# Re-ordering the hand-written start of a fused linear-attention and MLP kernel: unit order, fences, a split weight conversion and load order

## The chip, the cores and the metric

The kernel runs on one core of one Trainium2 chip. The metric is device time in microseconds (us); before the change the median of nine runs is 604.74 us (603.56 to 607.88). Engines are named as in the profile: PE is the matrix engine, PEld its weight loads, DVE the vector engine, ACT the scalar engine, POOL GpSimd, SP the engine that here only issues DMAs.

## What is computed

Two blocks one after the other, in float32:

```python
# r, k, v, w: (4, 8, 768, 48); u: (8, 48); state: (B, H, 48, 48), zero at first
for t in range(S):
    cur = einsum('bhd,bhe->bhde', u[None] * k[:, :, t], v[:, :, t])
    y[:, :, t] = einsum('bhd,bhde->bhe', r[:, :, t], state + cur)
    state = w[:, :, t][:, :, :, None] * state + einsum('bhd,bhe->bhde', k[:, :, t], v[:, :, t])
x = y.transpose(0, 2, 1, 3).reshape(3072, 384)
h = x @ w_in                                  # (3072, 2048)
out = (0.5 * h * (1 + erf(h / sqrt(2)))) @ w_out   # (3072, 384)
```

The two weight matrices arrive as 64-bit floats. The kernel converts them itself to 32-bit floats while it runs.

## The kernel before

**Tiles.** The 3072 tokens are eight tiles of 384, numbered x = 0 to 7. For each tile `attention(x, unit)` makes the tile's 384 x 384 input of the MLP, transposed (`xT`), and `mlp(x)` makes the tile's output. Tile 0 is cut into two units, each with half of the heads, so that work can start when half of its data is in; unit 0 is called U0 here and unit 1 U1. Every later tile is one unit. While the MLP of tile x - 1 runs on PE, the attention of tile x is woven into it.

**How the order is made.** Nothing is scheduled by a tool: the order of the Python calls is the order of the instructions on every engine. `attention` and `mlp` are generators. Each `next` on an attention emits one slot: slot 0 products with u (ACT, L367) and products of the decays (DVE, L377), slots 1 and 2 the level h = 1, slots 3 to 7 the levels h = 2, 4, 8, 16, 32, slot 8 the transposes of k (PE L572, copied by ACT L574), slot 9 the products k v (PE L598), then the part of y inside a chunk (PE L639), the chain of states (DVE L618 and L613), and the part of y from the states (PE L677). A level is a block of products `d` on PE (L408), a product on DVE that changes r and k in place (L443), and a masked copy of `d` into `a_sb` (DVE L453; for h = 16 and 32 ACT L450). A level's `d` needs the r and k that the level before it left. Between L639 and L677 stand the fences (L649 and L651): tiny DVE copies of the last columns of y, which make what follows wait for the first set of y products.

The units of tile 0 take turns: slots 0 to 2 for U0 and then U1, and then one slot for each in turn. From slot 8 on U1 goes first (`units.reverse()`). After slot 8 come one whole conversion, and then nine hand-ordered steps, (0, 0, 1, 0, 0, 1, 1, 0, 1), where 0 stands for U1 and 1 for U0. `keep_warm(n)` puts n bfloat16 matmuls of zeros on PE (L196), whose results nobody uses.

**End of tile 0.** U1's y goes to `xT` in two ways: one pair of heads is copied to `ysb` by ACT (L703) and spread by six small DMAs (L707, three on ACT's queue and three on SP's), the other by two DVE copies (L700). U0's y is copied by ACT and DVE (L684). When all of these are in, the first matmul of `mlp(0)` (L874, `h_ps`) can start.

**Weights.** Each matrix is cut into eight pieces of 768 values per partition: pieces 0 to 7 are of `w_in`, pieces 8 to 15 of `w_out` (called o0 to o7 here). A piece is loaded raw (five buffers), `prepare` makes its two halfway forms f and e on ACT (L297, L298; two buffers each), and `finish` makes the 32-bit weights with four DVE instructions (L309, L311, L312, L316). `conversion` does one piece: it prepares the piece after it, finishes its own, and issues the load of a further one. Two matmul steps of `mlp(0)` use one piece: steps 0 to 15 are the sixteen blocks of h (L874), two to a piece, and steps 16 to 31 the sixteen blocks of the output product of two row groups (L1011), block f of it at step 16 + f, with piece o0 for f = 0 and 1 and so on to o7 for f = 14 and 15.

**mlp(0) with attention(1).** For tile 1 three hand-written lists set the order by step: conversions after steps 0, 2, 4, 6, 8, 10, 12, 14, 15, 17, 18, 20, 22, 24; attention slots after steps 1, 3, 5, 7, 9, 11, 13 (levels), 15 (transposes), 18 (k v), 20 (the chain, twenty L613), 26 (L639 and fences), 32 (L677). In one step the conversion is emitted ahead of the slot. Two conversions stand ahead of step 0, so piece o5 (blocks f = 10 and 11) is converted after step 20, ahead of the chain that is emitted at the same step.

**Loads at the start.** SP issues tile 0's data first. `shares` then hands out loads slot by slot, each held back by a one-column DVE memset of its target (L130, L174): weight piece 0 in three parts, tile 1's r, k and w in eight shares (`load_second`), tile 1's v, then pieces 1 and 2 in three parts each. Piece 3 is loaded by the first conversion and piece 4 by the second.

The tile-1 step lists in the code:

```python
place = [1, 3, 5, 7, 9, 11, 13, 15, 18, 20, 26, 32] if x == 1 else [1, 6, 8, 13, 15, 16, 18, 18, 20, 21]
...
if x == 1 and step in (0, 2, 4, 6, 8, 10, 12, 14, 15, 17, 18, 20, 22, 24):
    convert()
```

Of the kernel before, what the change touches and what calls it, by code (L numbers as in the profile page):

```python
# [36 lines left out]
HALFWAY = 2  # L37


def as_float(bits):  # L40
    return struct.unpack("<f", struct.pack("<I", bits))[0]
# [3 lines left out]
def kernel(  # L45
# [25 lines left out]
    nc = tc.nc  # L71
# [25 lines left out]
    def units_of(x):  # L97
        return NPART if x == 0 else 1
# [22 lines left out]
    def load_v(x, dma):  # L121
        loaded[x][1] = io.tile([128, v.shape[2]], F32, name="v_in")
        dma.dma_start(out=loaded[x][1], in_=v[x])

    def load_second(dma):

        loaded[1] = [None, None]
        for i in range(SHARES):
            s = slice(i * 3 * ALL // SHARES, (i + 1) * 3 * ALL // SHARES)
            nc.vector.memset(bufs[1][:, s.start:s.start + 1], 0.0)  # L130
            dma.dma_start(out=bufs[1][:, s], in_=rkw[1, :, s])
            yield
        load_v(1, dma)
        yield

    def load(x, dma):

        if x >= NX:
            return
        loaded[x] = [None, None]  # L140
        for i in range(3):
            if i == 1:
                load_v(x, dma)
                yield
            t = bufs[x % 2 if i == 0 else 1]
            for j in range(3):
                a = i * ALL + j * ALL // 3
                dma.dma_start(out=t[:, a:a + ALL // 3], in_=rkw[x, :, a:a + ALL // 3])
                yield
# [12 lines left out]
    def weight_in(gate=False):  # L162

        if len(raws) < len(pieces):
            dst, src = pieces[len(raws)]
            raws.append(cv.tile([128, PIECE], I64, name="raw", bufs=AHEAD) if wide else None)
            if wide:
                dst = raws[-1].rearrange("p (a c) -> p a c", a=dst.shape[1])
            if not gate:
                nc.sync.dma_start(out=dst, in_=src)  # L170
                return
            for i in range(dst.shape[1]):
                if wide:
                    nc.vector.memset(dst[:, i].bitcast(U32)[:, 0:1], 0)  # L174
                nc.sync.dma_start(out=dst[:, i], in_=src[:, i])
                yield
# [13 lines left out]
    def keep_warm(n, elsewhere=False):  # L190
        if elsewhere:
            t = pd.tile([128, 2, BANK], F32, name="warm", tag="d")[:, 0]
        else:
            t = ps.tile([128, BANK], F32, name="warm", tag="mm", bufs=2)
        for _ in range(n):
            nc.tensor.matmul(t, lhsT=zeros[:, 0:128], rhs=zeros, start=True, stop=True)  # L196
# [72 lines left out]

    halfway, converted = [], [0]  # L270

    def conversion():

        i = converted[0]
        if i >= len(pieces):
            return
        converted[0] += 1

        prepare(i + HALFWAY)
        if wide:  # L280
            yield from finish(pieces[i][0], raws[i], *halfway[i])
        for _ in weight_in():
            pass

    def convert():
        for _ in conversion():
            pass

    def prepare(upto):
        if not wide:  # L290
            return
        for i in range(len(halfway), min(upto, len(raws))):
            words = raws[i].bitcast(U32).rearrange("p (a b) -> p a b", b=2)
            lo, hi = words[:, :, 0], words[:, :, 1]
            f = cv.tile([128, PIECE], U32, name="f")
            e = cv.tile([128, PIECE], U32, name="e")
            nc.scalar.activation(out=f.bitcast(F32), in_=hi.bitcast(F32), func=AF.Abs)  # L297
            nc.scalar.activation(out=e.bitcast(F32), in_=lo, func=AF.Identity, scale=2.0 ** -51, bias=two)  # L298
            halfway.append((f, e))

    def finish(dst, raw, f, e):

        hi = raw.bitcast(U32).rearrange("p (a b) -> p a b", b=2)[:, :, 1]

        nc.vector.tensor_scalar(out=f.bitcast(F32), in0=f.bitcast(F32), scalar1=as_float(0x38000000),  # L309
                                scalar2=as_float(0x47EFFFFF), op0=ALU.max, op1=ALU.min)  # L310
        nc.vector.tensor_scalar(out=f, in0=f, scalar1=3, scalar2=None, op0=ALU.logical_shift_left)  # L311
        nc.vector.scalar_tensor_tensor(out=e, in0=hi, scalar=0x80000000, in1=e,  # L312
                                       op0=ALU.bitwise_and, op1=ALU.bitwise_or)
        yield
        f, e = (z.rearrange("p (a c) -> p a c", a=dst.shape[1]) for z in (f, e))
        nc.vector.tensor_tensor(out=dst.bitcast(U32), in0=f, in1=e, op=ALU.add)  # L316
# [3 lines left out]
    def attention(x, unit):  # L320
# [288 lines left out]
        def chain_states():  # L609
            for c in range(NC - 1 + int(first)):  # L610
                if c or not first:
                    for q in range(qs):
                        nc.vector.scalar_tensor_tensor(out=stq[:, q, c], in0=stq[:, q, c - 1] if c else b4[:, q, NC - 1],  # L613
                                                       scalar=totq[:, q, c:c + 1], in1=kvs[q // Q][:, q % Q, c // 2, c % 2],
                                                       op0=ALU.mult, op1=ALU.add)
                else:
                    for b in range(np_):
                        nc.vector.tensor_copy(out=stq[:, b * Q:(b + 1) * Q, c], in_=kvs[b][:, :, 0, 0])  # L618
# [24 lines left out]
        def fences():  # L643

            for y, y_ps in ys:
                fence = wk.tile([128, 2], F32, name="fence")
                if split:
                    for c in range(2):
                        nc.vector.tensor_copy(out=fence[:, c:c + 1], in_=y[c][:, NI * C - 1:NI * C])  # L649
                else:  # L650
                    nc.vector.tensor_copy(out=fence, in_=y_ps[:, :, NI * C - 1])  # L651

        if x == 0:

            inside()
            yield
            chain_states()
            yield
            fences()
        else:  # L660
            chain_states()
            yield
            inside()
            fences()
            yield
# [44 lines left out]
    N_SLOTS = len(LEVELS) + 7  # L710
# [310 lines left out]


    units = [attention(0, unit) for unit in range(units_of(0))]
    second = load_second(nc.sync)
    shares = chain(weight_in(gate=True), second, weight_in(gate=True), weight_in(gate=True))
    for unit in units:
        for _ in range(3):
            next(unit)
# [3 lines left out]
    for slot in range(3, N_SLOTS - 4):  # L1032
        for _ in range(2):
            next(shares, None)
        if slot == N_SLOTS - 7:
            prepare(1)
        if slot == N_SLOTS - 5:

            units.reverse()
        for unit in units:  # L1040
            next(unit)
            keep_warm(2)
    for _ in shares:
        pass
    convert()

    for unit in (0, 0, 1, 0, 0, 1, 1, 0, 1):
        next(units[unit])
    keep_warm(6, True)
    convert()  # L1050
# [5 lines left out]
    for x in range(1, NX):  # L1056

        place = [1, 3, 5, 7, 9, 11, 13, 15, 18, 20, 26, 32] if x == 1 else [1, 6, 8, 13, 15, 16, 18, 18, 20, 21]
        place_next = [38, 47] if x == 1 else [21, 24] if x % 2 == 0 else [25, 27]
        loads = load(x + 1, nc.scalar if x > 1 else nc.sync)  # L1060

        times = range(20, 30) if x == 1 else (2, 3, 4, 5, 16, 17, 18, 19, 20, 21)
        following = attention(x + 1, 0) if x + 1 < NX else iter(())
        more = iter(())
        for step, _ in enumerate(mlp(x - 1)):
            if x == 1 and step == 2 * NF - 2:

                make_quarter_masks()
                more = w_sums()
            next(more, None)  # L1070
            if x == 1 and step in (0, 2, 4, 6, 8, 10, 12, 14, 15, 17, 18, 20, 22, 24):
                convert()
            if step in times:
                next(loads, None)
            while place and place[0] <= step:
                place.pop(0)
                next(slots, None)
            while place_next and place_next[0] <= step:
                place_next.pop(0)
                next(following, None)  # L1080
            if x == NX - 1:

                if step == 18:
                    more_h = h_sums()
                for _ in range({18: 1, 22: 2, 25: 1}.get(step, 0)):
                    next(more_h)
        for _ in slots:
            pass
        slots = following
# [62 lines left out]
```

## Time and profile before

| what | value |
|---|---|
| median of nine runs | 604.74 us |
| time of the profiled execution | 605.13 us |
| its span, first to last instruction | 603.3 us |
| PE busy | 587.2 us (97%) |
| DVE busy | 468.4 us (78%) |
| ACT busy | 178.9 us (30%) |
| granted PE clock | 1.000 |
| 31.6 to 45.5 us: PE, DVE, ACT busy | 9.37, 9.73, 5.14 of 13.90 us |
| 45.5 to 91.4 us: PE, DVE, ACT busy | 44.62, 45.02, 28.06 of 45.90 us |
| 91.4 to 115.6 us: PE, DVE, ACT busy | 24.20, 23.60, 10.47 of 24.20 us |
| 115.6 to 603.0 us: PE, DVE, ACT busy | 484.35, 363.12, 125.34 of 487.40 us |

All times of events count from the first instruction of the profiled execution. The first stretch is the end of tile 0's attention. The second holds the h matmuls of tile 0 with the levels of tile 1, the third the output matmuls of tile 0's first two row groups. The last stretch is all the rest. In the profile's own time lines a row has start, duration, engine, line, operation and tiles, a count, and in brackets the idle time of the engine before it with what ended that time.

### The profile page before, as it was taken

Reading aid. Unit: us, or ns where it says so; the run is one execution under the profiler, and the core shown is the slowest. Engines: PE = TensorE matmul, PEld = TensorE weight load, DVE = VectorE, ACT = ScalarE, POOL = GpSimd, SP = SyncE. Lnnn points to the kernel's source line nnn. Section 1 sums busy time; section 2 is a strip of 40 time slices with the busy share of each in tenths; the row PEclk is TensorE's granted clock in tenths of the full one; section 3 lists DMA queues with packets and bytes.
Section 4 is the critical chain, followed back from the end, with each engine's and each line's share of the span. In section 5 each row is a group of like instructions: output and inputs, shape, how many; then the busy total and the mean of one; then the engine's idle time right before and its main releaser. Section 6 shows DMA issues by size and latency. Waiting matters only on the chain.

```text
span 603.3 us, 16117 instructions
## 1 busy us (share of the span) xinstructions
PE 587.2 (97%) x6993; PEld 455.5 (76%) x7008; DVE 468.4 (78%) x896; ACT 178.9 (30%) x414; POOL 8.4 (1%) x24
## 2 busy tenths in 40 slices
PE   8769999999999999999999999999999999999997
PEld 4556666656699568986699568995789668999977
DVE  8969999998875978588884988679786888665701
ACT  2336477023222322203322232113222133024400
POOL 3100000000000000000000000000000000000000
PEclk9999999999999999999999999999999999999999
DMA  5767348002052304203052303313042002010000
GB/s 198 233 200 251 108 157 304 33 28 84 8 109 75 92 2 110 73 21 93 1 112 73 98 1 75 93 36 92 3 107 67 17 1 40 14 39 8 1 14 26
DMA packets 50566, 46.72 MB, mean 77 GB/s; under 512 B 31680, under 2 KB 35904, under 8 KB 50496
## 3 DMA queue, kind: packets, MB, share of 16 engines
q1 hardware_dynamic: 33152, 29.31, 15.8%
q10 hardware_dynamic: 17344, 16.39, 9.9%
q8 instruction: 55, 0.90, 0.6%
q14 instruction: 15, 0.12, 0.1%
HBM read 36.24 MB, written 4.72 MB: 68 GB/s over the span
## 4 chain that ended last, share of the span: by engine, by line
PE 91%; DVE 5%; issue 2%; DMA 1%; SPq 0%; ACT 0%
PE h_ps L874 35%; PE o_ps L888 31%; PE o_ps L1011 5%; PE b L828 5%; PE d L521 4%; PE kv_ps L598 2%; PE d L408 2%; PE y_ps L639 2%; PE y_ps L677 2%; PE o_ps L917 2%; DVE rkw L443 2%; DMA rkw<-in_rkw_dram 1%; DVE a_sb L453 1%; PE d L514 1%; DVE a_sb L419 1%
## 5 line engine op out<-in xcount | busy, mean ns | idle before, releaser
L874 PE MATMUL h_ps<-xT,w_in_sb 128*128 128x384 f32 x672 | 223.0, 489 | 0.0
L874 PEld LDWEIGHTS h_ps<-xT,w_in_sb 128*128 128x128 f32 x672 | 125.9, 190 | 84.6 <-ACT xT L684 0.4
L877 ACT ACTIVATE g<-h_ps 128x384 f32<-128x384 f32 (+1 forms) x112 | 49.3, 443 | 168.4 <-PE h_ps L874 168.4
L888 PE MATMUL o_ps<-t,s 128*128 128x192 f32 x480 | 81.9, 329 | 0.0
L888 PEld LDWEIGHTS o_ps<-t,s 128*128 128x128 f32 x480 | 77.8, 190 | 0.7
L552 DVE COPY_PREDICATED a_sb<-quarter,d 128x384 f32<-128x384 uint8 (+2 forms) x108 | 45.1, 438 | 2.5
L888 PE MATMUL o_ps<-w_out_sb,g 128*128 128x192 f32 x224 | 38.7, 326 | 0.0
L888 PEld LDWEIGHTS o_ps<-w_out_sb,g 128*128 128x128 f32 x224 | 37.0, 190 | 1.9
L1011 PE MATMUL o_ps<-w_out_sb,g 128*128 128x384 f32 x96 | 32.2, 491 | 0.0
L613 DVE SCALAR_TENSOR_TENSOR st<-st,tot_sb,kv_ps 128x48 f32<-128x48 f32 x160 | 29.0, 258 | 4.1 <-PE kv_ps L598 4.1
L408 PEld LDWEIGHTS d<-rkw 64*64 64x64 f32 x1152 | 18.8, 135 | 12.8 <-DVE rkw L443 7.3
L888 PE MATMUL o_ps<-w_out_sb,s 128*128 128x192 f32 x160 | 28.3, 330 | 0.0
L888 PE MATMUL o_ps<-t,g 128*128 128x192 f32 x160 | 27.6, 326 | 0.0
L1011 PEld LDWEIGHTS o_ps<-w_out_sb,g 128*128 128x128 f32 x96 | 17.7, 190 | 12.3 <-DVE o_sb L1017 0.6
L345 DVE TRANSPOSE_TENSOR_REDUCE rkw<-kx 128x48 f32<-128x1536 f32 (+3 forms) x24 | 26.8, 1156 | 0.2
L521 PEld LDWEIGHTS d<-kx,rkw 64*64 64x64 f32 x1152 | 24.3, 133 | 3.4 <-DVE a_sb L559 1.6
L521 PE MATMUL d<-kx,rkw 64*64 64x96 f32 x1152 | 26.5, 245 | 0.0
L888 PEld LDWEIGHTS o_ps<-t,g 128*128 128x128 f32 x160 | 26.3, 190 | 0.0
L888 PEld LDWEIGHTS o_ps<-w_out_sb,s 128*128 128x128 f32 x160 | 25.9, 190 | 0.4
L408 PE MATMUL d<-rkw 64*64 64x64 f32 (+1 forms) x1152 | 21.2, 222 | 5.1 <-DVE rkw L443 2.9
L534 DVE TENSOR_TENSOR rkw<-rkw,tot_sb 128x768 f32<-128x768 f32 x12 | 11.5, 958 | 17.3 <-PE d L521 17.3
L381 DVE TENSOR_TENSOR rkw<-rkw 128x384 f32<-128x384 f32 (+2 forms) x24 | 23.6, 1006 | 0.4
(148 smaller groups left out, 741.5 us busy)
## 6 DMA issues: line engine op xcount, KB each, us to landing
rkw<-in_rkw_dram ACTq DMA_DIRECT2D x45, 256.0 KB, 2.8
raw<-in_w_out_dram SPq DMA_DIRECT2D x8, 768.0 KB, 4.5
out_dram<-o_sb SPq DMA_DIRECT2D x21, 192.0 KB, 1.9
raw<-in_w_in_dram SPq DMA_DIRECT2D x5, 768.0 KB, 6.2
v_in<-in_v_dram ACTq DMA_DIRECT2D x5, 584.0 KB, 3.6
raw<-in_w_in_dram SPq DMA_DIRECT2D x9, 256.0 KB, 3.4
rkw<-in_rkw_dram SPq DMA_DIRECT2D x8, 288.0 KB, 3.8
rkw<-in_rkw_dram SPq DMA_DIRECT2D x9, 256.0 KB, 7.3
```

The lines of the kernel that those rows point to most:

```text
L345: nc.vector.tensor_reduce(out=fine_sb[:, e, 0:n].rearrange("p a n -> p (a n)"), in_=kx[:, o:o + n * n_m].rearrange("p (m j) -> p m j", j=3 ...
L381: nc.vector.tensor_mul(z, z, by)
L408: nc.tensor.matmul(d[half[p], g, n * width:(n + 1) * width], lhsT=kc[half[g], b, i, p], rhs=right(half[g], b, i, p), start=True, stop=True)
L443: nc.vector.tensor_mul(rk, rk, tt)
L521: nc.tensor.matmul(d[half[p], g, i * 3 * C // 2:(i + 1) * 3 * C // 2], lhsT=kc[half[g], (n + i) // NI, (n + i) % NI, p], rhs=rx[half[g], 2 ...
L552: nc.vector.copy_predicated(out=an[:, :, :, :, (a + 1) * h:], mask=mask.to_broadcast(data.shape), data=data)
L613: nc.vector.scalar_tensor_tensor(out=stq[:, q, c], in0=stq[:, q, c - 1] if c else b4[:, q, NC - 1], scalar=totq[:, q, c:c + 1], in1=kvs[q ...
L828: nc.tensor.matmul(o, lhsT=lhsT, rhs=rhs, start=start and i == 0, stop=(i == len(factors) - 1), skip_group_check=True)
L874: nc.tensor.matmul(h_ps, lhsT=w_in_sb[:, f // FI, j, f % FI * 128:(f % FI + 1) * 128], rhs=xT[:, j, :], start=(j == 0), stop=(j == NJ - 1))
L877: nc.scalar.activation(out=gs[group][:, f % FG, 0:t], in_=h_ps[:, 0:t], func=AF.Gelu)
L888: nc.tensor.matmul(o, lhsT=lhs(j), rhs=rhs(j), start=start and j == 0, stop=(j == HF - 1), skip_group_check=True)
L1011: nc.tensor.matmul(o, lhsT=block(i, f // HF, f % HF), rhs=w_out_sb[:, f, :], start=(f == 0), stop=(f == NF - 1))
```

## The change

- The units change places at slot 7 (h = 32) and no longer at slot 8, so U1's h = 32 stands ahead of U0's.
- In tile 0, the fences are emitted in the same step as the chain of states, right behind it. Before, they stood in the step after.
- The first conversion is cut in three: its first two DVE instructions (f) are emitted at slot 7 ahead of both units' L443, the third (e) after slot 8, and the fourth (the sum, which writes the weights) behind both units' chains and fences. With the fourth goes the load of piece 3. The preparation of piece 1 is moved behind the third instruction.
- The hand-ordered steps become (0, 0, 1), each followed by one warming matmul, then (0, 0, 1, 1), then the end of the conversion, then (0, 1). U1's last copies (L700) so come behind U0's chain and fences.
- Weight piece 1 is loaded ahead of tile 1's r, k and w. Tile 1's v is loaded by SP at the end, after all shares.
- In the loop for tile 1, the conversion after step 4 is dropped from the list and one after step 26 is added. Every piece from 4 on is so converted one entry later: piece 4 after step 6, o5 after step 22, o7 after step 26.

```diff
@@ load_second
-        load_v(1, dma)
-        yield
@@ conversion
-    def conversion():
+    def conversion(ahead=True):
...
-        prepare(i + HALFWAY)
+        if ahead:
+            prepare(i + HALFWAY)
@@ finish
         nc.vector.tensor_scalar(out=f, in0=f, scalar1=3, scalar2=None, op0=ALU.logical_shift_left)
+        yield
         nc.vector.scalar_tensor_tensor(out=e, in0=hi, scalar=0x80000000, in1=e,
                                        op0=ALU.bitwise_and, op1=ALU.bitwise_or)
@@ attention, x == 0
             chain_states()
-            yield
             fences()
+            yield
@@ start
-    shares = chain(weight_in(gate=True), second, weight_in(gate=True), weight_in(gate=True))
+    shares = chain(weight_in(gate=True), weight_in(gate=True), second, weight_in(gate=True))
...
-        if slot == N_SLOTS - 5:
+        if slot == N_SLOTS - 6:
             units.reverse()
+            piece = conversion(ahead=False)
+            next(piece)
         for unit in units:
             next(unit)
             keep_warm(2)
     for _ in shares:
         pass
-    convert()
-    for unit in (0, 0, 1, 0, 0, 1, 1, 0, 1):
+    load_v(1, nc.sync)
+    next(piece)
+    prepare(HALFWAY)
+    for unit in (0, 0, 1):
+        next(units[unit])
+        keep_warm(1)
+    for unit in (0, 0, 1, 1):
+        next(units[unit])
+    for _ in piece:
+        pass
+    for unit in (0, 1):
         next(units[unit])
     keep_warm(6, True)
     convert()
@@ loop, x == 1
-            if x == 1 and step in (0, 2, 4, 6, 8, 10, 12, 14, 15, 17, 18, 20, 22, 24):
+            if x == 1 and step in (0, 2, 6, 8, 10, 12, 14, 15, 17, 18, 20, 22, 24, 26):
                 convert()
```

More of the change, by code (lines that the diff above doesn't have):

```diff
@@ L657, in attention @@
             chain_states()
+            fences()
             yield
-            fences()
         else:
```

## The prediction

> **What bounds the kernel now.** I read the page's slices first, then the time lines of PE and DVE over the first 130 us. The slices:
>
> ```profile
> PE   8769999999999999999999999999999999999997
> DVE  8969999998875978588884988679786888665701
> ```
>
> A slice is 15.1 us. PE is the bound from slice 3 on; whatever delays it there is not won back. Slices 0 to 2 are tile 0's attention, which nothing overlaps. In slices 3 to 7 DVE is as full as PE. The end of tile 0 on PE, and then on DVE (start, duration, row):
>
> ```profile
> 34.10 0.92 PE L598 MATMUL kv_ps<-v_in,kx 64*64 64x48 f32 x48
> ...
> 35.55 0.63 PE L598 MATMUL kv_ps<-v_in,kx 64*64 64x48 f32 x31
> 38.78 0.45 PE L598 MATMUL kv_ps<-v_in,kx 64*64 64x48 f32 x17 [2.60 <-issue]
> ...
> 42.77 1.38 PE L677 MATMUL y_ps<-rkw,st 64*64 64x64 f32 x40 [1.67 <-DVE fence L649]
> 44.09 1.47 PE L196 MATMUL warm<-zeros 128*128 128x512 bf16 x5
> 45.53 4.11 PE L874 MATMUL h_ps<-xT,w_in_sb 128*128 128x384 f32 x12
> ```
> ```profile
> 39.30 0.26 DVE L618 COPY st<-kv_ps 128x96 f32<-128x96 f32 x1 [1.94 <-PE kv_ps L598]
> 39.59 1.84 DVE L613 SCALAR_TENSOR_TENSOR st<-st,tot_sb,kv_ps 128x48 f32<-128x48 f32 x10
> 41.34 1.12 DVE L700 COPY xT<-y_ps 48x384 f32<-48x384 f32 x2
> 42.49 0.22 DVE L649 COPY fence<-y_ps 128x1 f32<-128x1 f32 x2
> 44.19 1.12 DVE L684 COPY xT<-y_ps 48x384 f32<-48x384 f32 x2 [1.47 <-PE y_ps L677]
> 45.34 0.56 DVE L309 TENSOR_SCALAR f<-f 128x768 f32<-128x768 f32 x1
> ```
>
> PE stops inside a run of equal matmuls and waits for nothing on another engine: it waits for its own instructions. Counting weight loads, its two such pauses (26.92 and 36.17) stand 255 loads, 510 instructions, apart. The trace's packets of the instruction queue (16 KB each) start at 24.58, 30.99, 36.42, 39.91. The third takes 0.97 us, and PE goes on 1.39 us after its end. Behind the pause hang L618, the chain, L700, the fence, L677 and L684, up to the first h matmul at 45.53. Of tile 0's MLP with tile 1, from PE and DVE:
>
> ```profile
> 67.10 1.60 PE L408 MATMUL d<-rkw 64*64 64x32 f32 x96 [0.64 <-DVE rkw L443]
> ...
> 73.41 1.60 PE L408 MATMUL d<-rkw 64*64 64x32 f32 x96 [0.64 <-DVE rkw L443]
> ...
> 96.94 10.59 PE L1011 MATMUL o_ps<-w_out_sb,g 128*128 128x384 f32 x32
> 107.45 1.63 PE L639 MATMUL y_ps<-a_sb,v_in 64*64 64x64 f32 x96
> ```
> ```profile
> 100.51 0.55 DVE L309 TENSOR_SCALAR f<-f 128x768 f32<-128x768 f32 x1
> ...
> 103.44 3.58 DVE L613 SCALAR_TENSOR_TENSOR st<-st,tot_sb,kv_ps 128x48 f32<-128x48 f32 x20
> 106.94 0.55 DVE L309 TENSOR_SCALAR f<-f 128x768 f32<-128x768 f32 x1
> ...
> 112.78 0.22 DVE L651 COPY fence<-y_ps 128x2 f32<-128x2 f32 x2
> ```
>
> Between 45.34 and 112.78 DVE waits for nobody (its waits in that stretch are empty). It sets the pace: piece o7 is done at 112.8, and PE uses it at about 113.0.
>
> [...] 48-matmul groups last 0.7 us here, so a block is gone in about 2 us, and its fetch took 4.7 (34.10 to 38.78). [...] the loads moved 307 GB/s over 34.0 to 38.8, and the packet started 2.3 us after PE entered its block. [...] The trace shows clock 1.00 over 31.6 to 45.5 in spite of the 2.60 pause.
>
> **The change, part by part.** Estimates, worked from the rows above.
>
> *Swap at slot 7.* U1's d (h = 32) needs U1's L443 (27.88 + 0.95). Placed first it starts at 28.9, where U0's started at 28.31. Then pitch 1.39 twice: U1's transposes at 31.67 instead of 31.80. Gain 0.1, and kv of U1 at 34.0. The two f instructions (1.1) ahead of L443 lie in DVE's idle 0.46 and 0.44 and U1's slack; e (0.95) ends by 33.2 and L618 of U1 starts at about 35: nothing; without that cover they would cost their 1.1.
>
> *Loads.* Piece 1 comes some 10 us sooner; ACT's 1.09 wait for it at 35.67 had nothing urgent behind it. Tile 1's data (landing 3.1 to 5.3) is out by 32.3, so in by 38, needed at 46.9; its v is needed at 95. Piece 3's load moves from 33.98 behind SP's three xT DMAs, to about 42.7, landing 4.1 to 7.0 later; ACT prepares it at 49.47, DVE takes it at 53.8. Nothing; 0.3 at worst. Nothing moves past POOL's queue.
>
> *Three warming matmuls.* 0.25 each (0.52 for two). Two lie ahead of the block boundary, which PE so reaches at 36.4; the fetch hides them. The third delays U1's L677 by 0.25.
>
> *The fetch.* Block entered at 34.0. From entry to the packet's start four fetches of this stage took 1.2, 3.5, 2.3, 1.1: mean 2.0. Go-on: 34.0 + 2.0 + 0.97 + 1.39 = 38.4 (before 38.78). Best, as in the quiet at 43.85, 0.35: 36.7; worst 39.9.
>
> *Fences and copies.* From 38.4: kv ends, warm, L677 of U1 at 38.95, U0's inner y ends at 41.0 (before: 39.05, 41.1). The chain is over at 40.8, so the fence takes 41.05 to 41.27; L677 of U0 ends at 42.75; DVE meanwhile L316 0.93 and L700 1.1 to 43.3, then L684 to 44.45. The small DMAs land at about 44.5 (third ACT issue 42.5 + 2.2 before, 0.1 sooner). DVE takes up the second conversion at 44.45 instead of 45.34, PE the h matmuls at 44.65: **gain 0.9** (0 to 2.5).
>
> *The list.* Let t count from that conversion's start. A conversion is 2.93 (L309 to L309, 50.89 to 53.82), L443 1.66, L453 1.68 at h = 2 and 0.88 at h = 4 and 8. Without the conversion of step 4, L443 of step 5 starts at 17.1, when PE's d of that step ends, not at 20.0. Both 0.64 pauses go. But piece 4 now follows that level: 17.1 + 1.66 + 1.68 + 3.05 = 23.5. PE wants it for h block 8 at 22.6, waits 0.9, and starts block 8 at 23.5 (before 68.63 - 45.34 = 23.3). From here they alternate: DVE's L443 of steps 9 and 13 wait for PE's d (29.25 and 40.6), 1.4 of idle time that it did not have. Then six conversions in a row from 42.3, less one: o0 to o4 end at 56.9, the chain takes 3.5 to 60.4, and o5 is done at 63.4. PE: transposes at 44.5, outputs 16 to 18 at 45.8, kv at 49.7, step 19 at 51.3, seven steps of 1.31 to step 26 at 60.5. Step 26 is block f = 10, which needs o5: **a wait of 2.9**. Behind it on PE are the rest of the step and L639, and the fences wait for L639, then L677 of tile 1 for the fences. L639 follows at 64.75, before at 107.45 - 45.34 = 62.1: **cost 2.65**. o6 (66.3, wanted 67.6) and o7 (69.3, wanted 70.2) come in time. Later DVE trails PE by less than before, so nothing is given back: PE is 99% busy from 115.6.
>
> *Sum.* 2.65 - 0.9 = +1.75. The profiled execution's span 603.3 becomes 605.05, its time 605.13 becomes 606.9. The median shown is 0.39 under that execution: 604.74 + 1.75 = **606.5**.
>
> **Rivals.**
>
> *The list pays (faster).* The pauses of 1.28 go, and DVE is far enough ahead at step 26 that o5 costs nothing: -0.9 - 1.3 = -2.2, 602.5. For: both pauses are real, and the dropped conversion stood right ahead of them. Against: DVE has no idle time before step 26 in which to get ahead; it would have to be 2.9 earlier against PE.
>
> *The fetch comes promptly (no change).* Fewer loads are outstanding at 34.0, since piece 3 has left. Go-on at 36.7, L677 of U1 at 37.3, L684 done at 42.8: gain 2.5, sum +0.15, 604.9. Against: four gated loads and v are issued just then, about 1.6 MB from 32.3 on.
>
> *The clock drops (slower).* [...] If the clock halves for one window of about 3.4 us, half of it is lost: +1.7, sum 3.45, 608.2. [...] Against: 2.60 did not do it.
>
> **How the numbers follow.** My case 0.60 (606.5; own range 605.5 to 607.3 by the fetch), list pays 0.08, prompt fetch 0.15, clock 0.17. A measurement can tell about 0.3%, 1.81 us, from no change: 602.93 and 606.55. My case lies on that edge, half of it on either side. Slower 0.17 + 0.30 = 0.47, same 0.15 + 0.30 = 0.45, faster 0.08. The range leaves out the faster rival and the far end of the clock: 604.4 to 608.1.
>
> **What would show it.** The pause in U0's kv ending at 37 to 39; L677 of U0 right behind the fence, with L700 under it; first h matmul near 44.6; no L443 wait at the levels h = 4 and 8, but one of about 0.9 on L316 at h block 8; DVE idle ahead of L443 twice; and about 2.9 us of PE idle inside the sixteen L1011 after kv, released by L316. If that wait is absent, or the h matmuls start before 43, I am wrong.

## The result and the profile after

The changed kernel takes 608.29 us in the median of 17 runs (607.11 to 612.06), against 604.33 us in 54 runs of the kernel before on the same chips. The ratio is 1.0068, interval [1.0053, 1.0084]: some 4.0 us slower. The prediction had the sign right, at 606.5, but the time lies just above its range, which ended at 608.1.

The profiled execution after took 611.07 us with a span of 609.3, so it is one of the dearer ones; its losses are larger than the median's 4.0. The slices of the page:

```profile
PE   8798999899999999999999999999999999999997
PEclk9998999999999999999999999999999999999999
```

A slice is 15.2 us. Slice 2 is fuller than before (9 for 6), so the end of tile 0 is shorter. But slice 3, which was a 9, is now an 8, and there the granted clock falls to an 8 as well. These are the places to look at. First the start, on PE (start, duration, row, idle time before it):

```profile
36.40 0.55 PE L598 MATMUL kv_ps<-v_in,kx 64*64 64x48 f32 x19 [0.28 <-issue]
...
39.59 0.80 PE L677 MATMUL y_ps<-rkw,st 64*64 64x64 f32 x20 [0.32 <-DVE fence L649]
40.95 0.80 PE L677 MATMUL y_ps<-rkw,st 64*64 64x64 f32 x20 [0.56 <-issue]
...
43.12 4.11 PE L874 MATMUL h_ps<-xT,w_in_sb 128*128 128x384 f32 x12
47.16 1.49 PE L408 MATMUL d<-rkw 64*64 64x32 f32 x88
50.21 0.32 PE L408 MATMUL d<-rkw 64*64 64x32 f32 x8 [1.57 <-issue]
50.46 5.83 PE L874 MATMUL h_ps<-xT,w_in_sb 128*128 128x384 f32 x12
```

And on DVE:

```profile
41.78 1.12 DVE L684 COPY xT<-y_ps 48x384 f32<-48x384 f32 x2 [0.34 <-PE y_ps L677]
42.94 0.56 DVE L308 TENSOR_SCALAR f<-f 128x768 f32<-128x768 f32 x1
```

The start does what the change says: the fence follows the chain, L677 of U0 waits 0.32 for it where it waited 1.67, and the first h matmul comes at 43.12 instead of 45.53. Of these 2.4 us, 0.3 had come before anything was changed (the level products that first wait for the masked copy L453 start at 16.11 after, at 16.42 before), so 2.1 belong to the new order and to the fetch in the kv products, which now stops PE for 0.28 instead of 2.60. In these two profiles nearly all of it is the fetch: from where PE goes on in the kv products to the first h matmul it takes 6.75 before (38.78 to 45.53) and 6.72 after (36.40 to 43.12), where a second pause for instructions, of 0.56, stands inside U0's L677.

Then PE stops in the middle of the first products d of tile 1, at 47.16: 1.57 us, released by no engine. That is again PE waiting for its own instructions: the packet of them starts at 47.84 and ends at 48.75, and PE goes on 1.46 after that. The pauses stand one packet of instructions apart: from the matmul at 36.40 to the one at 40.95 the trace's rows hold 128 matmuls, 256 instructions with their weight loads, and 255 more PE instructions of the trace lie between there and 50.21. On the page 6996 matmuls and 7011 weight loads share 55 packets of 16 KB, 255 to a packet. Such a run of 256 is called a block here. The next 12 h matmuls take 5.83 us instead of 4.11. The view by stretches shows what runs meanwhile (length, busy time of PE, PEld, DVE, ACT, POOL with counts, granted clock, DMA share, GB/s):

```profile
41.04:47.84 6.80, 6.64 (x85) 3.95 (x85) 6.25 (x10) 5.96 (x10) 0.00 (x0) 1.00 0.86 270
47.84:50.87 3.03, 1.46 (x65) 1.23 (x58) 2.88 (x7) 1.41 (x3) 0.00 (x0) 1.00 1.05 400
50.87:54.28 3.41, 3.41 (x7) 1.87 (x6) 3.34 (x5) 0.00 (x0) 0.00 (x0) 0.50 0.84 275
```

In the first stretch the packet has not started yet: PE still has instructions, and the DMA engines are busy for 0.86 of the time. In the second PE works half of the time, while the DMA engines are full (1.05). In the third, of 3.41 us, the clock is 0.50. By 54.28 nothing is left of the gain: aligned by the same matmul, the execution after is 2.4 ahead at the first h block, 0.6 ahead behind the pause, and 1.0 behind after the stretch at half clock.

The list, on PE and then on DVE:

```profile
70.06 4.11 PE L874 MATMUL h_ps<-xT,w_in_sb 128*128 128x384 f32 x12 [1.01 <-DVE w_in_sb L316]
74.10 1.60 PE L408 MATMUL d<-rkw 64*64 64x32 f32 x96
...
110.03 1.56 PE L1011 MATMUL o_ps<-w_out_sb,g 128*128 128x384 f32 x4 [2.87 <-DVE w_out_sb L316]
111.51 1.63 PE L639 MATMUL y_ps<-a_sb,v_in 64*64 64x64 f32 x96
```
```profile
75.77 1.76 DVE L443 TENSOR_TENSOR rkw<-rkw,tot_sb 128x1536 f32<-128x1536 f32 x1 [0.40 <-PE d L408]
...
87.17 1.76 DVE L443 TENSOR_TENSOR rkw<-rkw,tot_sb 128x1536 f32<-128x1536 f32 x1 [1.12 <-PE d L408]
```

Both pauses of 0.64 ahead of d are gone. In their place PE waits 1.01 for piece 4 and 2.87 for piece o5, both released by the last instruction of a conversion. DVE, which had no idle time there, now has 0.40 and 1.12. L639 comes at 111.51, before at 107.45: 4.1 behind.

The rest of the 6.0 us of span is lost later, in the kv products: 0.7 at tile 2 and 1.2 at tile 4. Behind the first four of them PE waits until the last blocks of k have been moved (the DMAs rkw<-kx, L468). On PE, tile 4:

```profile
316.77 1.69 PE L598 MATMUL kv_ps<-v_in,rkw 64*64 64x48 f32 x92 [1.07 <-issue]
```

The row names no releaser, but the last of these moves lands at 316.68, just ahead of it. The profile of before has no such wait at tile 2 and some 0.3 at tile 4.

### The profile page after: what moved, and what is told of

Read it like the earlier page. It is cut to its first block, busy times and chain, and to the rows that moved or that the text cites. A ratio compares the mean times of both kernels' runs of the same rounds, so it can differ in the third digit from the quotient of the medians.

```text
span 609.3 us, 16126 instructions
## 1 busy us (share of the span) xinstructions
PE 591.0 (97%) x6996; PEld 457.4 (75%) x7011; DVE 468.5 (77%) x896; ACT 178.7 (29%) x414; POOL 8.4 (1%) x24
## 4 chain that ended last, share of the span: by engine, by line
PE 70%; DMA 1%; issue 0%; DVE 0%; ACTq 0%
PE o_ps L888 29%; PE h_ps L874 26%; PE b L828 5%; PE d L521 4%; PE o_ps L917 2%; PE kv_ps L598 2%; PE y_ps L639 2%; PE y_ps L677 1%; DMA rkw<-kx 1%; PE d L514 1%; DVE o_sb L960 0%; ACTq L468 0%
## 5 line engine op out<-in xcount | busy, mean ns | idle before, releaser
L888 PE MATMUL o_ps<-w_out_sb,s 128*128 128x192 f32 x160 | 28.3, 330 | 0.0
L345 DVE TRANSPOSE_TENSOR_REDUCE rkw<-kx 128x48 f32<-128x1536 f32 (+3 forms) x24 | 26.8, 1157 | 0.2
L521 PE MATMUL d<-kx,rkw 64*64 64x96 f32 x1152 | 26.5, 245 | 0.0
```

The source lines that it names most:

```text
L345: nc.vector.tensor_reduce(out=fine_sb[:, e, 0:n].rearrange("p a n -> p (a n)"), in_=kx[:, o:o + n * n_m].rearrange("p (m j) -> p m j", j=3 ...
L521: nc.tensor.matmul(d[half[p], g, i * 3 * C // 2:(i + 1) * 3 * C // 2], lhsT=kc[half[g], (n + i) // NI, (n + i) % NI, p], rhs=rx[half[g], 2 ...
L888: nc.tensor.matmul(o, lhsT=lhs(j), rhs=rhs(j), start=start and j == 0, stop=(j == HF - 1), skip_group_check=True)
```

## Experiments

Each ratio is against runs of the kernel before on the same chip, with its 95% interval; it can differ from the quotient of the two medians by some 0.0008. The first four take the change apart; the rest test what the first four left.

**The list alone.** Before, with only the new list of conversions:

```diff
-if x == 1 and step in (0, 2, 4, 6, 8, 10, 12, 14, 15, 17, 18, 20, 22, 24):
+if x == 1 and step in (0, 2, 6, 8, 10, 12, 14, 15, 17, 18, 20, 22, 24, 26):
```

> The kernel before with the new list of conversion steps alone. Theory A (the list costs what was worked out, and the rest of the loss is the start: PE's instructions fetched late behind pieces 3 to 5, and the clock at half for one window): +2.65 us against before, ratio 1.0044, with a PE wait of about 2.9 us on L316 inside the output matmuls. Rival B (the list is the whole loss): +4.0, ratio 1.0066. Rival C (the list is harmless): -1.3, ratio 0.998.

Measured: 608.96 (6 runs), 1.0077 [1.0047, 1.0107], some 4.6 us: by the time alone nearer to rival B than to theory A. Its profile has the same waits as after, 1.00, 0.17 and 2.87. The last one:

```profile
109.78 2.86 PE L1011 MATMUL o_ps<-w_out_sb,g 128*128 128x384 f32 x4 [2.87 <-DVE w_out_sb L316]
```

Four output matmuls take 2.86 instead of 1.56: the clock is 0.50 from 109.88 to 113.29, right behind the wait. So the list costs its waits, and in some executions (four of the six) the clock on top.

**The start alone.** After, with the old list:

```diff
-if x == 1 and step in (0, 2, 6, 8, 10, 12, 14, 15, 17, 18, 20, 22, 24, 26):
+if x == 1 and step in (0, 2, 4, 6, 8, 10, 12, 14, 15, 17, 18, 20, 22, 24):
```

> The changed kernel with the old list of conversion steps. Theory A: the first h matmul stays at about 43.1 us (2.4 sooner than before), but the pause of 1.6 us inside the first d of tile 1 stays, and with it in most runs the half clock for 3.4 us: sum between -0.6 and +1.1 us against before, ratio 0.999 to 1.002. Rival B: with the old list only the gain is left, -2.4, ratio 0.996. Rival C: the start is the whole loss, +4, ratio 1.0066.

Measured: 605.72 (14 runs), 1.0015 [1.0001, 1.0029]. That is inside theory A's range. The new start is no gain; it costs about 0.9, with an interval from 0.1 to 1.8. Its profile shows the first h matmul at 43.56 and the fetch in kv at 0.56, so the gain is made, and then lost. This execution has no pause in d; it has late kv products at tile 2 (0.73) and at tile 6 (0.61).

**Piece 3 loaded as early as before.** After, with the whole load of piece 3 right ahead of tile 1's v:

```diff
+    for _ in weight_in():
+        pass
     load_v(1, nc.sync)
```

> The changed kernel with weight piece 3 loaded right behind the shares and ahead of tile 1's v, about as early as in the kernel before, instead of at the end of tile 0. Theory A: one load fewer stands in front of the instruction fetch at 41 to 48 us, so the pause inside the first d of tile 1 shrinks or goes, the clock stays at 1.0, and the time falls by 1.8 to 3.5 us against the changed kernel, to +0.5 to +2.2 against before (ratio 1.001 to 1.004). Rival: the fetch is not held by that load, +4.0 (1.0066), pause and half clock as in the changed kernel.

Measured: 610.58 (5 runs), 1.0102 [1.0089, 1.0116]. It is dearer than either expectation, so the theory that the early load would give the start its gain back fell. The pause in d has gone, but it has only moved forward, into U0's L677:

```profile
43.34 0.80 PE L677 MATMUL y_ps<-rkw,st 64*64 64x64 f32 x20 [2.75 <-issue]
```

The packet of instructions that ends this pause starts at 40.82; in after the same one starts at 38.65. The first h matmul comes at 45.51, as late as before the change.

**Pieces 3 and 4 both early, old list.** Two such loads ahead of tile 1's v:

```diff
+    for _ in weight_in():
+        pass
+    for _ in weight_in():
+        pass
     load_v(1, nc.sync)
-(0, 2, 6, 8, 10, 12, 14, 15, 17, 18, 20, 22, 24, 26)
+(0, 2, 4, 6, 8, 10, 12, 14, 15, 17, 18, 20, 22, 24)
```

> The changed kernel with the old list of conversion steps and with weight pieces 3 and 4 both loaded right behind the shares. Theory A: no pause inside the first d of tile 1, clock 1.0, and only the gain at the start is left: -2.4 us against before, ratio 0.996. Rival: piece 5 alone is enough to hold the fetch, or the two loads now hold the fetch inside kv of U0 as in the kernel before: -0.6 to +1.1, ratio 0.999 to 1.002.

Measured: 606.94 (10 runs), 1.0040 [1.0020, 1.0061], again dearer than either expectation. One more load ahead, and the pause is longer still:

```profile
44.29 1.33 PE L677 MATMUL y_ps<-rkw,st 64*64 64x64 f32 x20 [3.57 <-issue]
```

Its packet starts at 41.80, 5 us after PE entered the block ahead of it (36.72); the clock is 0.50 from 42.86 to 49.68. In these profiles the pause follows the loads: it stands at the fetch that comes while large loads are under way (piece 3 and tile 1's v in the third experiment, pieces 3 and 4 and v here), and with one more of them it is 3.57 instead of 2.75. That is one execution of each.

**Three warming matmuls fewer, old list.** This tests whether the late kv waits come from where the 256-instruction blocks end: with `keep_warm(3, True)` for `keep_warm(6, True)` the instructions from there on lie in their blocks as before the change.

```diff
-    keep_warm(6, True)
+    keep_warm(3, True)
-(0, 2, 6, 8, 10, 12, 14, 15, 17, 18, 20, 22, 24, 26)
+(0, 2, 4, 6, 8, 10, 12, 14, 15, 17, 18, 20, 22, 24)
```

> The changed kernel with the old list, and with three instead of six warming matmuls ahead of the first h matmul, so that from there on PE's instructions stand at the same places of their 256-instruction blocks as in the kernel before. Theory A (the waits of kv of tiles 2, 4 and 6, which the kernel with the old list showed and the kernel before did not, come from the shift of six instructions): they go, -2.0 to -2.4 us against before, ratio 0.9965. Rival B (they come from the DMA queues, whatever the blocks): they stay, +0.5 to +1.3, ratio 1.0015.

Measured: 604.82 (22 runs), 1.0008 [0.9992, 1.0023]: no difference from before, as rival B had it. The profile still has a late kv wait (0.51 at tile 2), which speaks against block ends as their cause. It also has the pause in d, with the packet at 49.72 and the three loads at 42.91, 43.56 and 44.15:

```profile
52.04 0.43 PE L408 MATMUL d<-rkw 64*64 64x32 f32 x5 [1.76 <-issue]
```

**The opposite shift on the kernel before:**

```diff
-    keep_warm(6, True)
+    keep_warm(9, True)
```

> The kernel before with nine instead of six warming matmuls ahead of the first h matmul: six instructions more ahead of everything that follows. They cost 0.65 us there themselves. Theory A (the shift brings the late waits): waits in kv of tiles 2, 4 or 6, +1.7 to +2.7 us, ratio 1.003 to 1.0045. Rival B (it doesn't): +0.65, ratio 1.001.

Measured: 604.86 (14 runs), 1.0015 [0.9996, 1.0034]. The interval holds rival B's 1.001 and nothing of theory A's 1.003 or more but its edge, so the shift alone is worth little. Its profile shows something else: with the old start the kv products had no pause at all, and d had one of 0.91, its packet at 46.98.

**The list alone, with the wait filled.** The first experiment, and twelve bfloat16 matmuls of zeros in front of the output block that waits:

```diff
+            if x == 1 and step == 25:
+                keep_warm(12, True)
```

> The kernel before with the new list and twelve warming matmuls (2.6 us) in front of output block 10, where PE waits 2.9 us for its weights. Theory A (the idle time itself is what halves the clock in most runs of the list alone): the clock stays at 1.0, the wait stays as time, +2.2 to +2.9 us against before, ratio 1.004 to 1.005, some 2 us below the list alone. Rival B (the clock falls for another reason, or the wait alone is dearer): +4.6 as the list alone, ratio 1.0077.

Measured: 607.58 (6 runs), 1.0046 [1.0029, 1.0064], with the mean clock at 0.999 or more in all six. The wait for o5 is still there, only PE is busy in it. So the list's waits are worth 2.8 us by the ratio (1.7 to 3.9 by its interval; the medians differ by 3.2), and the other 1.8 of the first experiment's 4.6 is put down to the clock, which four of its six runs had lost and none of these.

**The loads cut up and held back, old list, three warming matmuls.** Pieces 4 and 5 are loaded in three parts, each behind a one-column DVE memset of its target:

```diff
 # conversion
-        for _ in weight_in():
+        for _ in weight_in(gate=i in (1, 2)):
-    keep_warm(6, True)
+    keep_warm(3, True)
-(0, 2, 6, 8, 10, 12, 14, 15, 17, 18, 20, 22, 24, 26)
+(0, 2, 4, 6, 8, 10, 12, 14, 15, 17, 18, 20, 22, 24)
```

> The kernel with the old list and three warming matmuls, and the loads of weight pieces 4 and 5 each held back in three parts by memsets behind DVE's second and third conversion, so that of the big loads piece 3 alone stands in front of PE's instruction fetches at the end of tile 0. Theory A (those fetches are held by the big loads): no pause above 0.6 us of PE between 36 and 52 us, clock at 1.0 in nearly all runs, -2.0 to -2.4 us against before, ratio 0.9965, with less spread than the same kernel without the gates. Rival B: piece 3 alone holds the fetch, or the gates cost DVE more than they save: -1.3 or worse, ratio 0.998 to 1.001.

Measured: 602.56 (8 runs, 601.79 to 603.80), 0.9966 [0.9953, 0.9979]. This version beats both kernels. It differs from the fifth experiment, which was level, in the gates alone. Only piece 3 leaves at 41.52, the six parts from 46.15 on; the packet of instructions starts at 41.54, and d runs through:

```profile
43.27 4.11 PE L874 MATMUL h_ps<-xT,w_in_sb 128*128 128x384 f32 x12 [1.06 <-DVE xT L684]
47.31 1.60 PE L408 MATMUL d<-rkw 64*64 64x32 f32 x96
```

There is no late kv wait, and the mean clock is 0.999 or more in all eight.

**The changed kernel with the gates only.** The one line of `conversion` above, the new list kept:

> The changed kernel with nothing altered but the loads of weight pieces 4 and 5, which are held back in three parts each by memsets behind DVE's second and third conversion. Theory A (in the changed kernel three big loads in a row hold PE's next instruction block, which costs a pause of 1.6 us and, in many runs, a window of half clock): no pause in the first d of tile 1, the list's wait of 2.9 us stays, and with it half clock in a part of the runs: -2.3 + 2.8 + 0 to 1.7, +0.5 to +2.2 us against before, ratio 1.001 to 1.0035. Rival B (the loads matter only together with the old list): +4.0, ratio 1.0066.

Measured: 608.21 (15 runs), 1.0053 [1.0035, 1.0072]. That is between the two expectations, and lower than the changed kernel's 1.0068 by less than the noise. The first h matmul comes at 41.76 and d has no pause, as theory A had it. But the list's wait remains, and the clock falls: it is 0.50 from 104.42, before the wait has ended, to 111.24:

```profile
105.22 2.93 PE L1011 MATMUL o_ps<-w_out_sb,g 128*128 128x384 f32 x4 [2.88 <-DVE w_out_sb L316]
```

In 10 of its 15 runs the mean clock is at or below 0.997. With the pause in d gone, the list's wait alone is enough to lose the clock.

**The same, with the twelve matmuls in the wait.** Gates and `keep_warm(12, True)` at step 25:

> The same, and twelve warming matmuls in front of output block 10, where PE waits for its weights. Theory A: the clock stays at 1.0 in all runs, -2.3 + 2.8 = +0.5 us against before, ratio 1.001; this is the changed kernel with fetch and clock taken out, so what is left is its gain at the start and the price of its list. Rival B (the warming matmuls cost as much as they save): as without them, 1.003.

Measured: 606.44 (22 runs), 1.0031 [1.0018, 1.0044], clock 0.999 or more in all 22. The clock behaves as expected, the time does not: +1.9 where about +0.5 was expected. That is as much as rival B gave, but not for its reason, since without the filling the same kernel stands at 1.0053. Its profile has late kv waits at tiles 2, 4 and 6 (0.30, 0.72, 0.56), which this expectation had not counted.

**The kernel before with the gates only:**

> The kernel before with the loads of pieces 4 and 5 held back in the same way, nothing else. Theory A (the gates pay because the changed start would otherwise put three big loads in front of a fetch; the start before has piece 3 out by 34 us): between 0 and -0.5 us, ratio 0.999 to 1.000. Rival B (the gates alone are the gain of the kernel with old list, three warming matmuls and gates): -2.0, ratio 0.9966.

Measured: 603.43 (22 runs), 0.9990 [0.9973, 1.0006]. By themselves the gates are worth about 0.6, and the interval includes nothing at all. So most of the eighth experiment's gain needs the new start and the gates together, though the two intervals overlap from 0.9973 to 0.9979.

## Why the prediction was right or wrong

**The list: right.** "A wait of 2.9" measured 2.87, the 0.9 on piece 4 measured 1.01, the 1.4 of new idle time on DVE 1.52, both pauses of 0.64 went, and L639 did not get back in time. "Cost 2.65" measured 2.8 (1.7 to 3.9) where the clock is kept out (the seventh experiment). DVE sets the pace there, and a conversion moved behind the chain of states is late by its own length (2.93 from L309 to L309 before; the wait is 2.87).

**Swap, fences, copies: right in order, smaller in size.** The fence, L677 and L684 came in the order that was worked out, and the second conversion starts 1.16 after the start of L684, as before. From where PE goes on in the kv products to the first h matmul, 38.4 to 44.65 makes 6.25, against 6.75 before. The start alone and the eighth experiment take 6.40 (37.16 to 43.56) and 6.39 (36.88 to 43.27), so the new order is worth some 0.35. After itself takes 6.72, with the pause of 0.56 at the next end of a block in it, for which the prediction had no term.

**The fetch in kv: its term rested on one execution.** "Go-on: 38.4" measured 36.40, the prompt case of the rivals. Against the one profile of before this makes 2.1 instead of 0.9. But the pause of 2.60, from which the gain was counted, is not what the old start always has. Five executions of it show 2.60, 2.33, 1.51, 0.41 and none; eight of the new start show at most 0.56 in the kv products. Counted from the same level products (those that first wait for L453) to the first h matmul, the old start takes 29.1, 29.8, 27.4 and 26.9, mean 28.3; with the execution of the nine warming matmuls (26.4, with the 0.65 of the three that were added taken off) the mean is 27.9. The new start, leaving out the two kernels that put loads ahead of it, takes 27.0, 27.0, 28.1, 26.5, 26.2 and 26.2, mean 26.8. That is an estimate of 1.1 to 1.5 gained, not far from the 0.9, over a spread that one profile could not show.

**The failed step: "Loads".** "Piece 3's load moves from 33.98 ... to about 42.7 ... Nothing; 0.3 at worst." Its data were indeed not late. What the step left out is who stands behind it. The load now leaves at 41.04, and those of pieces 4 and 5 at 41.66 and 42.27: 2.3 MB within 1.3 us. PE enters its next block of instructions at 40.95. The packet of 16 KB for the block after that one starts at 47.84, 6.9 us later, and ends at 48.75; PE goes on at 50.21. Before, the packet started at 43.85 and d had no pause. For the fetch in kv the prediction had set the loads (307 GB/s) beside the late packet (2.3 us); of the next fetch it did not ask the same. PE lives 7.7 us on the block that it enters at 40.95, until 48.64; with 0.91 for the packet and 1.46 from its end until PE goes on, the packet had to start within about 5.3 us, an estimate from these rows. It took 6.9. In the ninth experiment, with the gates, it took 4.4 (39.59 to 43.99), and d had no pause. How late the packet is differs between executions: in the start alone it came at 42.53, in spite of loads at 41.80 and 42.47, and in the sixth experiment the old start had a pause in d too. What the step cost is shown with the old list and three warming matmuls: the gates take 604.82 to 602.56, some 2.3 us. In the changed kernel itself they are worth about 0.9 (1.0068 to 1.0053), within the noise, and there the list's wait still takes the clock in 10 of 15 runs; gates and filled wait together (1.0031) take off 2.2, clear of the noise.

**The clock: named as a rival, and given too little.** Of the 112 executions of the kernel before that ran beside the experiments, 20 have a mean clock at or below 0.997; of the 18 of the changed kernel, 12. In the kernel before, such executions take 606.10 in the median and the others 604.29; in after 609.47 and 607.70. So one loss costs about 1.8 there, near half of 3.41 us; in the second, fifth and ninth experiments the same difference is 0.8, 2.2 and 1.0. For one loss the prediction reckoned +1.7 from "one window of about 3.4 us"; in after the clock is at 0.50 for 3.41 us, and the twelve h matmuls in which that falls take 1.72 more (5.83 for 4.11). When it falls is less plain. In after it falls twice, at 50.87 and, behind the last instruction, at 610.66: 559.79 apart, which is 164 times 3.4133, while the trace gives the stretch at half clock as 3.413; in the fourth and ninth experiments half clock lasts 6.82, twice that. This does not prove a fixed step. If the step is taken as fixed, an estimate from these figures, it cuts every profile that has a fall (the tenth experiment's has none) into stretches of 3.4133, and on that count a fixed length of wait does not decide. In after a stretch ends at 108.9, in the middle of the wait for o5 (107.16 to 110.03): 1.74 of idle time lie in it, and no half clock followed. In the list alone the stretch that ends at 109.88 holds the whole wait of 2.87, and half clock followed. "2.60 did not do it" falls to the same count: from the fall at 604.60 back, a stretch of before ends at 37.98, inside the pause from 36.18 to 38.78, so that 1.81 lie on one side and 0.79 on the other. Counted so from 30 us on, every stretch at full clock with 2.07 us or more without a matmul was followed by half clock (2.07, 2.27, 2.46 and 2.87 in the ninth, third, fourth and first experiment), and of those with less only the two with the pause in d were (1.57 in after, 1.67 in the fifth experiment), while others with as much, up to 1.81, were not. What sets these two apart is not shown. Nor is it shown that the length of a wait alone decides, as the prediction weighed it: gaps of 1.57 and 2.87 did it here, and one of 2.60 did not.

**The sum.** Among executions at full clock, after stands at 607.70 and before at 604.29: +3.4. The list gives 2.8 of it by the seventh experiment. The start alone gives 0.7 (605.00 against 604.29). Together 3.5, which agrees within the noise. The prediction had 2.65 - 0.9 = 1.75: the list is where it was put, and the start is 1.6 worse. The clock adds the remaining 0.5 to the median, since most executions after lose some of it (12 of 18) and most before do not (20 of 112 do). The tenth experiment says it from the other side: with the loads held back and the clock kept, the changed kernel costs 1.9 (1.1 to 2.7), near the prediction's 1.75, a sum that holds nothing for the loads and nothing for the clock.

**What stays open.** The late kv products of tiles 2, 4 and 6 wait 0.4 to 1.6 us in all in single executions of every kernel with the new start but the eighth experiment's, and in some with the old. The moves of k land later against the kv products there, but why was not found; the theory of the block ends is not supported, since they remain with the old alignment. So the loss at the start is shown to be undone by gates (604.82 to 602.56), but only in part how it divides: in the fifth experiment the 11 of 22 executions at full clock take 603.47 in the median, so about 1.4 of the 2.3 go with the clock, and 0.9 are left for the pause in d and the late kv products. Nor was shown what holds the packet back inside the DMA engines, only that it mostly starts late when several large loads are under way, and that the pause moves when they are moved. The earlier load of piece 1 and the later one of tile 1's v were not tried by themselves.

## What to carry to other kernels

PE's instructions came in here as one more transfer beside the loads, 55 packets of 16 KB. Where many tiny matmuls use up a block of 256 instructions in about 2 us (here 96 products d, 192 instructions with their weight loads, last 1.60), look which bulk loads leave just then, and hold these back in parts, behind a stage that has slack; here that took 604.82 to 602.56. Price a conversion or copy that is moved behind a chain by the wait at its first user, and add the clock to a PE wait as a chance: the list's wait of 2.9 cost it in 14 of 21 runs, and in these profiles 1.57 was the shortest that cost it, while 2.60 did not. A pause of a few us in one profile may be one of a wide spread; before counting a gain from it, see whether it is there in others.

## What was not expected of the hardware

Counted from PE's entry into the block ahead, a packet of 16 KB of instructions took from 0.4 us (43.46 to 43.85, before) to 6.9 (40.95 to 47.84, after) to start, in one stage of the two kernels. And twelve bfloat16 matmuls of zeros in a wait of 2.9 us (2.75 us busy) kept the mean clock at 0.999 or more in 28 of 28 runs of two kernels, where without them it was 0.997 or less in 14 of 21 runs.
